# Banded attention in blocks of 32 queries by 64 keys instead of 64 by 96

## The chip, the cores and the metric

The kernel runs on one core of a Trainium2 chip. The metric is the time of one execution in microseconds on the device. A core has TensorE (PE in the profile; its weight loads are PEld), VectorE (DVE), ScalarE (ACT), GpSimd (POOL) and SyncE (SP), which issues the transfers here.

## What is computed

Attention with a band mask, then two mixing blocks on its output:

```python
scores = scale * np.matmul(q, k.transpose(0, 1, 3, 2))          # 4 batches, 8 heads, 576 positions, 64 dims
mask_plain = (rel >= 0) & (rel < window)                        # window 32, heads 0 to 3
mask_dil = (rel >= 0) & (rel < window * dilation) & (rel % dilation == 0)   # dilation 4, heads 4 to 7
...
attn = np.exp(scores - max); attn = attn / (sum + 1e-09); x = attn @ v
...
k = np.maximum(xk @ w_k, 0.0); v = k * k @ w_v; r = sigmoid(xr @ w_r); y = r * v    # xk, xr: x mixed with the row before
...
u = y + (y.T @ U @ V).T; out = u + np.maximum(u @ w_ch1, 0.0) @ w_ch2
```

A query sees at most 32 keys: itself and the 31 before it (in the dilated heads, every fourth position).

## The kernel before

The program records all its operations with a length in ns and what each reads and writes, and `plan` (lines 127 to 280) puts them in an order for each engine by simulating them as a list scheduler does. So a changed operation can move any other one.

The attention is cut into 32 units: a batch, a part of the sequence (320 or 256 positions) and a pair of heads. The first four units run alone (`attend`), the other 28 in 14 pairs (`attend2`): 6 pairs of the first part, with five windows a unit, and 8 of the second, with four. A window is 64 queries (QW) by 96 keys (KW). A pair goes through these steps:

- `qk` (line 654): scores, per unit x, window w and head e one fp32 matmul with 64 rows (the head's dims), 64 columns of weights (queries) and 96 moving columns (keys). Head e goes to PSUM bank `sc[e]`, a window to the upper or lower 64 partitions, so four 64x64 tiles of the array are in use. `attend` does the same with two tiles (line 545).
- `low` (665): VectorE adds the mask, scales and takes the row minimum, 96 columns an instruction; `exp` (673): ScalarE; `inv` (679, 680): VectorE; `norm` (684): GpSimd, one instruction a head.
- `tr` (699): each slot of 128 queries by 96 keys is transposed, five or four for each of the two heads. `copy` (351): ScalarE brings them from PSUM to SBUF, 512 columns and, with five windows, 128 more for each head.
- `pv` (716): per unit, window and head one matmul with 96 rows (keys), 64 columns of weights (V) and 64 moving columns (queries), in two tiles of 128x64. Then ScalarE copies the unit's output into x.

q and k come in one transfer a unit (line 522), V in another (525, 96 rows). A loop over the chunks of the first mixing block (`quanta`, three-pass matmuls at lines 816 to 818; the first chunk in fp32 at 813 and 829) calls `visit(2)` at two places a chunk, which starts the next pair's scores and ends the last pair's; so the attention's matmuls lie in groups among those of the mix. The fp32 matmuls of the first chunk need weights that VectorE and ScalarE convert from 64-bit words (lines 384 to 391). After some 300 us the attention is done, and the second mixing block (lines 1037 to 1116) follows.

Of the kernel before, what the change touches and what calls it, by code (L numbers as in the profile page):

```python
# [25 lines left out]
QW, KW = 64, 96  # L26
PARTS = ((0, 320), (320, 576))
WINDOWS = (5, 4)

NMASK = 6  # L30

TWO = ((0, 1), (0, 2), (3, 4))
NALL = NMASK + len(TWO)


def unit_kind(pair, part):

    if part == 0:
        return 5, 320, (0, 32, 96, 160, 224), (0, 1, 1, 1, 1) if pair < 2 else (0, 2, 3, 4, 5)
    if pair < 2:  # L40
        return 4, 288, (0, 64, 128, 192), (1, 1, 1, 1)
    return 4, 384, (0, 96, 192, 288), (1, 1, 1, 1)
# [34 lines left out]
def tile_attention_mix_channel(  # L77
    ctx: ExitStack, tc: tile.TileContext, qk0, qk1a, qk1b, v0, v1, cst, mu, w1raw, w2raw, upk, vpk, out
# [35 lines left out]
    def bank(tag):  # L114

        return Lazy([P, 512], F32, tag, f"ps{tag}", 4, ps)
# [394 lines left out]
    def a_load(u, which=("qk", "v")):  # L511
        b, part, pair = unit(u)
        nw, kc = unit_kind(pair, part)[:2]
        if part == 0:
            src, vsrc = qk0[b * NPAIR + pair], v0[b * NPAIR + pair]
        else:
            src, vsrc = (qk1a if pair < 2 else qk1b)[b * 2 + pair % 2], v1[b * NPAIR + pair]
        if u not in raws:
            raws[u] = Lazy([P, QKW + VW], F32, "raw", "raw", 4)
        raw = raws[u]  # L520
        if "qk" in which:
            load(P * 4 * (nw * QW + kc), lambda: nc.sync.dma_start(raw()[:, : nw * QW + kc], src),
                 (raw, "qk"), lambda: raw())
        if "v" in which:
            load(KW * 4 * 2 * nw * D, lambda: nc.sync.dma_start(raw()[:KW, QKW : QKW + 2 * nw * D], vsrc),
                 (raw, "v"), lambda: raw()[:, QKW:])

    def attend(u):
        b, part, pair = unit(u)
        nw, kc, starts, mk = unit_kind(pair, part)  # L530
        raw = raws.pop(u)
        sc, pr = bank("S"), Lazy([P, 512], F32, "pr", "pr", 4)
# [3 lines left out]
        t0, t1 = PARTS[part]  # L536
        fifth = slice(t1 - t0, t1 - t0 + P)
        pts = Lazy([P, 5 * P], F32, "pt", "pts", 2)

        def qk():  # L540
            for w in range(nw):
                for e in range(2):
                    r = slice(e * D, (e + 1) * D)
                    k0 = nw * QW + starts[w]
                    nc.tensor.matmul(
                        sc()[e * QW : (e + 1) * QW, w * KW : (w + 1) * KW],
# [3 lines left out]
        pe(nw * 168, qk, [(raw, "qk")], [(sc,)], "qk")  # L550
        yield

        def low():
            for w in range(nw):
                c = slice(w * KW, (w + 1) * KW)
                nc.vector.tensor_tensor_reduce(
                    out=pr()[:, c], in0=sc()[:, c], in1=masks[mk[w]], scale=-0.125, scalar=1.0e38,
                    op0=ALU.add, op1=ALU.min, accum_out=mn()[:, w : w + 1],
                )

        op("DVE", nw * 177, low, [(sc,), ("cst",)], [(pr,), (mn,)], 170)

        def exp():
            for w in range(nw):
                c = slice(w * KW, (w + 1) * KW)
                nc.scalar.activation(
                    pr()[:, c], pr()[:, c], AF.Exp, bias=mn()[:, w : w + 1], scale=-1.0, accum_out=sm()[:, w : w + 1]
                )

        op("ACT", nw * 360, exp, [(pr,), (mn,)], [(pr,), (sm,)], 190, mode="exp")  # L570

        def inv():
            nc.vector.tensor_scalar(sm()[:, :nw], sm()[:, :nw], 1e-9, None, op0=ALU.add)
            nc.vector.reciprocal(sm()[:, :nw], sm()[:, :nw])

        op("DVE", 260, inv, [(sm,)], [(sm,)], 80)

        def norm():
# [817 lines left out]
```

## Time and profile before

| | us |
|---|---|
| median of 3 runs | 775.47 (772.08 to 777.58) |
| the profiled execution | 775.23 |
| its span, first to last instruction | 773.3 |
| TensorE busy | 740.0 (96%) |
| VectorE busy | 580.5 (75%) |
| ScalarE busy | 404.8 (52%) |
| GpSimd busy | 396.1 (51%) |

The profile is of one execution. Busy time is the union of an engine's instructions; matmuls overlap in the pipeline, so what one costs is read from the start of one to the start of the next. The trace counts two records for an fp32 matmul and one for a transpose.

### The profile page before, as it was taken

The numbers are of one execution on the slowest core, as the hardware profiler recorded it, in microseconds if no ns is written. First come the engines' busy times: TensorE is split into PE (matmuls) and PEld (weight loads), VectorE is DVE, ScalarE is ACT, GpSimd is POOL, SyncE is SP. The second block draws the span as 40 slices with busy tenths as digits, with TensorE's granted clock in tenths as the row PEclk, the third lists the DMA queues.
The fourth block names the chain that finished last, engine by engine and source line by source line (L and its number), as shares of the span: only waits on it lengthen the run. The fifth ranks groups of instructions, "written<-read, shape, count | busy, mean of one in ns | idle before, by whom it ended". The sixth has DMA issues, their size and how long they took to land. (4 is left out here: it accounts for less than half of the span.)

```text
span 773.3 us, 16141 instructions
## 1 busy us (share of the span) xinstructions
PE 740.0 (96%) x5784; PEld 678.2 (88%) x5784; DVE 580.5 (75%) x1302; ACT 404.8 (52%) x1019; POOL 396.1 (51%) x404
## 2 busy tenths in 40 slices
PE   4798999999999999999999999999999999999998
PEld 3566899999999999999898899889988999898986
DVE  5889989999999963556467889876797974665632
ACT  4578778767767765454345444443544343333310
POOL 1333236455646564355367668544677754455600
PEclk9989999999999999999999999999999999999999
DMA  8677627759685720345652344123442312032001
GB/s 251 207 230 227 202 71 236 231 169 288 207 271 177 235 90 31 106 129 178 202 196 79 103 155 141 54 89 97 144 135 69 122 56 82 29 110 82 28 1 54
DMA packets 54255, 107.56 MB, mean 139 GB/s; under 512 B 5920, under 2 KB 16032, under 8 KB 54176
## 3 DMA queue, kind: packets, MB, share of 16 engines
q1 hardware_dynamic: 54176, 106.54, 42.8%
q8 instruction: 45, 0.74, 0.4%
q14 instruction: 34, 0.28, 0.1%
HBM read 83.97 MB, written 22.54 MB: 138 GB/s over the span
## 5 line engine op out<-in xcount | busy, mean ns | idle before, releaser
L346 POOL TENSOR_TENSOR cl<-sums,ch 128x512 fp32r<-128x512 f32 x72 | 99.6, 1383 | 82.5 <-ACT ch L351 57.2
L1116 PE MATMUL psS<-hl,rh 128*128 128x512 f32 (+1 forms) x320 | 119.5, 373 | 2.0 <-DVE hl L1052 2.0
L1114 PE MATMUL psS<-hh,rh 128*128 128x512 f32 (+1 forms) x320 | 119.5, 374 | 1.7 <-ACT hh L1051 0.9
L1115 PE MATMUL psS<-hh,rl 128*128 128x512 f32 (+1 forms) x320 | 119.0, 372 | 0.0
L351 ACT ACTIVATE ch<-sums 128x512 fp32r<-128x512 f32 (+1 forms) x104 | 57.1, 561 | 113.3 <-DVE sums L471 104.7
L816 PE MATMUL psM<-xk,wh 128*128 128x288 f32 x336 | 101.2, 301 | 0.4 <-DVE y L878 0.4
L817 PE MATMUL psM<-xk,wl 128*128 128x288 f32 x336 | 99.1, 295 | 0.0
L818 PE MATMUL psM<-xk,wh 128*128 128x288 f32 x336 | 98.8, 294 | 0.0
L471 DVE TENSOR_TENSOR sums<-st 128x256 f32<-128x256 f32 (+1 forms) x144 | 90.5, 675 | 8.7 <-POOL cl L346 5.9
L346 POOL TENSOR_TENSOR cl<-st,ch 128x256 fp32r<-128x256 f32 x80 | 68.8, 876 | 54.6 <-PE psM L1039 31.4
L346 POOL TENSOR_TENSOR xk<-m,xk 128x288 fp32r<-128x288 f32 x56 | 52.4, 949 | 50.6 <-ACT xk L351 39.9
L1116 PEld LDWEIGHTS psS<-hl,rh 128*128 128x128 f32 x320 | 60.3, 188 | 14.0 <-DVE hl L1052 2.4
L1114 PEld LDWEIGHTS psS<-hh,rh 128*128 128x128 f32 x320 | 60.3, 188 | 12.2 <-DVE us L950 1.1
L346 POOL TENSOR_TENSOR k2s<-k,k2s 128x288 fp32r<-128x288 f32 x49 | 44.0, 900 | 48.8 <-ACT k2s L351 47.5
L1115 PEld LDWEIGHTS psS<-hh,rl 128*128 128x128 f32 x320 | 60.3, 189 | 9.5
L816 PE MATMUL psM<-k2s,wh 128*128 128x288 f32 x224 | 67.5, 301 | 0.0
L817 PE MATMUL psM<-k2s,wl 128*128 128x288 f32 x224 | 66.0, 295 | 0.0
L818 PE MATMUL psM<-k2s,wh 128*128 128x288 f32 x224 | 65.9, 294 | 0.0
L816 PEld LDWEIGHTS psM<-xk,wh 128*128 128x128 f32 x336 | 63.0, 188 | 1.4 <-DVE y L878 0.9
L818 PEld LDWEIGHTS psM<-xk,wh 128*128 128x128 f32 x336 | 63.2, 188 | 0.0
L817 PEld LDWEIGHTS psM<-xk,wl 128*128 128x128 f32 x336 | 63.1, 188 | 0.1
L1074 DVE TENSOR_TENSOR ok<-ok,psM 128x256 f32<-128x256 f32 (+1 forms) x96 | 46.4, 503 | 20.3 <-PE psM L1039 18.5
(156 smaller groups left out, 2146.8 us busy)
## 6 DMA issues: line engine op xcount, KB each, us to landing
st<-w2f SPq DMA_DIRECT2D x96, 256.0 KB, 3.1
w<-w2raw SPq DMA_DIRECT2D x32, 512.0 KB, 5.2
w<-w1raw SPq DMA_DIRECT2D x20, 512.0 KB, 5.2
w2f<-w SPq DMA_DIRECT2D x32, 256.0 KB
raw<-qk SPq DMA_DIRECT2D x16, 320.0 KB, 4.5
ytmp<-y SPq DMA_DIRECT2D x32, 144.0 KB, 2.1
yb<-ytmp SPq DMA_DIRECT2D x4, 1152.0 KB, 6.4
uf<-us SPq DMA_DIRECT2D x32, 144.0 KB, 2.4
```

The costliest lines, as they stand in the source:

```text
L346: op("POOL", t, lambda: nc.gpsimd.tensor_tensor(out=out_(), in0=a(), in1=b(), op=ALU.subtract), r, w, 40, lock=True)
L351: act(n, lambda: nc.scalar.activation(out_(), in_(), AF.Copy), r, w, psum, strided)
L471: dve(k * Q, lambda: nc.vector.tensor_tensor(out=q(sm_, n, k)(), in0=a(), in1=b(), op=op_), [(s1,), (s2,)], [(sm_, key)], two=True)
L816: nc.tensor.matmul(a, lhsT=wh, rhs=xh, start=start, stop=False)
L817: nc.tensor.matmul(a, lhsT=wl, rhs=xh, start=False, stop=False)
L818: nc.tensor.matmul(a, lhsT=wh, rhs=xl, start=False, stop=stop)
L1074: dve(k * Q, lambda: nc.vector.tensor_tensor(out=out_(), in0=a(), in1=b(), op=op_), r, w, two=True, psum=True)
L1114: nc.tensor.matmul(a, lhsT=wh, rhs=xh, start=(j == 0 and e == 0), stop=False)
L1115: nc.tensor.matmul(a, lhsT=wl, rhs=xh, start=False, stop=False)
L1116: nc.tensor.matmul(a, lhsT=wh, rhs=xl, start=False, stop=(j == 7 and e == 1))
```

## The change

A window is 32 queries by 64 keys, so a unit has ten or eight. Scores go to 64x32 tiles (four windows of a head side by side on the 128 partitions), a slot of 128 queries holds four windows, and two slots of 64 keys make one 128x128 transpose that holds blocks of both units. The keys of unit 0 then stand on partitions 0 to 63 and those of unit 1 on 64 to 127, so PV runs in 64x64 tiles, and a pair's V comes in one transfer, unit 0's windows above unit 1's. The last two windows of a unit with ten share a slot between the heads; their masked minimum takes two instructions on 64 partitions each. Units that run alone transpose three blocks and copy them once, 384 columns wide. The masks are 5 x 64 columns in place of 9 x 96, so the constants' transfer is 448 columns instead of 992. The lengths that `plan` counts with are changed along with it.

```diff
-QW, KW = 64, 96
+QW, KW = 32, 64
...
-        return 5, 320, (0, 32, 96, 160, 224), (0, 1, 1, 1, 1) if pair < 2 else (0, 2, 3, 4, 5)
+            return 10, 320, (0,) + tuple(range(0, 288, 32)), (0, 1, 1)
...
 def attend(u):
-        copy(4 * P, lambda: pts()[:KW, : 4 * P], lambda: pt()[:KW], [(pt,)], [(pts, 0)], psum=True)
-        if nw == 5:
-            copy(P, lambda: pts()[:KW, 4 * P :], lambda: ov()[:KW, fifth], [(ov, "t")], [(pts, 1)], psum=True)
+        copy(3 * P, lambda: pts()[:, : 3 * P], lambda: pt()[:, : 3 * P], [(pt,)], [(pts, 0)], psum=True)
...
 def attend2(ua, ub):
-        raw = [raws.pop(ua), raws.pop(ub)]
+        rq, rv = raws.pop(("qk", ua // 2)), raws.pop(("v", ua // 2))
...
-                        sc[e]()[h * QW : (h + 1) * QW, slot * KW : (slot + 1) * KW],
-                        lhsT=raw[x]()[r, w * QW : (w + 1) * QW], rhs=raw[x]()[r, k0 : k0 + KW], start=True, stop=True,
-        pe(nw * 4 * 60, qk, [(x, "qk") for x in raw], [(x,) for x in sc], "qk")
+                        s_, h = (w // 4, w % 4) if w < 8 else (2, 2 * e + w - 8)
+                        c = (2 * s_ + x) * KW
+                            sc[e]()[h * QW : (h + 1) * QW, c : c + KW], lhsT=rq()[r, q0 : q0 + QW],
+                            rhs=rq()[r, k0 : k0 + KW], start=True, stop=True,
+        pe(nw * 4 * 28, qk, [(rq, x * QKW) for x in range(2)], [(x,) for x in sc], "qk")
...
+                for i in range(4):
+                    low(sc[e](), i * KW, pr(), base + (first_ + i) * KW, mk[i // 2], mn[e](), first_ + i)
+                if nw == 10:
+                    for f in range(2):
+                        low(sc[f](), (4 + e) * KW, pr(), base + own * KW, mk[2], mn[e](), own, head(f))
...
-                nc.tensor.transpose(dst, pr[e]()[:, w * KW : (w + 1) * KW], ident)
+                nc.tensor.transpose(to(i), pr()[:, i * P : (i + 1) * P], ident)
...
-            copy(4 * P, lambda e=e: pts[e]()[:KW, : 4 * P], lambda e=e: pt[e]()[:KW], [(pt[e],)], [(pts[e], 0)], psum=True)
+        copy(4 * P, lambda: pts()[:, : 4 * P], lambda: pt(), [(pt, 0), (pt, 1)], [(pts, 0)], psum=True)
...
-                        lhsT=raw[x]()[:KW, c : c + D], rhs=pts[e]()[:KW, slot * P + h * QW : slot * P + (h + 1) * QW],
+                        r = slice(x * D, (x + 1) * D)
+                            ov[x]()[e * D : (e + 1) * D, w * QW : (w + 1) * QW], lhsT=rv()[r, n : n + D],
+                            rhs=pts()[r, c : c + QW], start=True, stop=True,
```

The order of TensorE's instructions before, from the second pair of units on (psS is a PSUM bank of the attention, psM one of the mix, wx a converted weight, pr the exponentials, pts their transposes; an `x` counts matmuls):

```order
L813 MATMUL psM<-xk_248,wx 128x288 x16
L699 MATMUL psS<-cst_t,pr 96x128 x8
L716 MATMUL psS<-pts,raw 64x64 x16
L654 MATMUL psS<-raw 64x96 x20
...
L813 MATMUL psM<-k_615,wx 128x288 x16
L699 MATMUL psS<-cst_t,pr 96x128 x10
L716 MATMUL psS<-pts,raw 64x64 x20
```

And the same place now:

```order
L812 MATMUL psM<-xk_284,wx 128x288 x16
L714 MATMUL psS<-cst_t,pr 128x128 x4
L732 MATMUL psS<-pts,raw 64x32 x32
L676 MATMUL psS<-raw 32x64 x40
...
L714 MATMUL psS<-cst_t,pr 128x128 x5
L732 MATMUL psS<-pts,raw 64x32 x40
```

The groups keep their turn; a group has half the transposes and twice the score and PV matmuls, each with fewer columns.

ScalarE's first instructions before (x is the attention's output, w a raw weight):

```order
L566 ACTIVATE pr,sm<-pr,mn 128x96 x5
L384 ACTIVATE wx<-w_99 128x512
L351 ACTIVATE pts<-psS 96x512
L384 ACTIVATE wx<-w_132 128x512
L566 ACTIVATE pr,sm<-pr,mn 128x96 x5
L351 ACTIVATE pts<-psS 96x128
L351 ACTIVATE x_94<-psS 128x320
```

And now:

```order
L546 ACTIVATE pr,sm<-pr,mn 128x64 x5
L385 ACTIVATE wx<-w_99 128x512
L352 ACTIVATE pts<-psS 128x384
L385 ACTIVATE wx<-w_144 128x512
L546 ACTIVATE pr,sm<-pr,mn 128x64 x5
L352 ACTIVATE x_94<-psS 128x320
```

Unit 0's second copy of transposes, which stood behind the exponentials of unit 1, is gone.

## Rows read from the trace of the kernel before

**Rows 1.** The page's part 1: busy time, share of the span, instructions

```profile
PE 740.0 (96%) x5784; PEld 678.2 (88%) x5784; DVE 580.5 (75%) x1302; ACT 404.8 (52%) x1019; POOL 396.1 (51%) x404
```

**Rows 2.** Windows: length, busy time (instructions) of each engine, granted clock, DMA share, GB/s

```profile
0.00:20.00 20.00, 9.96 (x93) 7.96 (x94) 10.44 (x48) 10.21 (x39) 3.51 (x9) 0.89 0.81 251
...
60.00:270.00 210.00, 203.87 (x2010) 193.61 (x2009) 199.39 (x557) 156.12 (x454) 104.31 (x118) 1.00 0.67 210
270.00:360.00 90.00, 88.83 (x731) 86.20 (x729) 50.22 (x107) 49.87 (x115) 46.73 (x55) 1.00 0.30 98
```

**Rows 3.** Groups of TensorE by form: count, busy us, mean ns, idle before

```profile
L716 PE MATMUL psS<-pts,raw 96*64 96x64 f32 x496 | 19.3, 231 | 3.3 <-ACT pts L351 3.3
...
L699 PE MATMUL psS<-cst_t,pr 128*96 128x128 f32 x124 | 16.2, 273 | 2.9 <-POOL pr L684 2.9
...
L654 PE MATMUL psS<-raw 64*64 64x96 f32 x496 | 14.3, 258 | 0.0
```

**Rows 4.** Timeline of TensorE around three pairs: start, busy us, records

```profile
241.54 1.39 PE L716 MATMUL psS<-pts,raw 96*64 96x64 f32 x40
242.86 1.06 PE L654 MATMUL psS<-raw 64*64 64x96 f32 x40
243.84 0.40 PE L816 MATMUL psM<-k2s,wh 128*128 128x288 f32 x1
...
256.74 1.25 PE L699 MATMUL psS<-cst_t,pr 128*96 128x128 f32 x10
...
278.69 1.15 PE L716 MATMUL psS<-pts,raw 96*64 96x64 f32 x32
279.78 0.89 PE L654 MATMUL psS<-raw 64*64 64x96 f32 x32
280.60 0.40 PE L816 MATMUL psM<-k2s,wh 128*128 128x288 f32 x1
```

**Rows 5.** Timeline of TensorE, the second block's 128x128 transposes

```profile
510.89 0.60 PE L909 MATMUL psM<-cst_t,yb 128*128 128x128 f32 x4
```

**Rows 6.** Timeline of TensorE, units that run alone

```profile
22.51 1.04 PE L545 MATMUL psS<-raw 64*64 64x96 f32 x20
23.48 0.80 PE L603 MATMUL psS<-pts,raw 96*64 96x64 f32 x20
```

**Rows 7.** Timeline up to 221.71 us (PE) and 221.76 us (PEld), a score group's first records

```profile
221.68 0.31 PE L654 MATMUL psS<-raw 64*64 64x96 f32 x4
...
221.68 0.21 PEld L654 LDWEIGHTS psS<-raw 64*64 64x64 f32 x8
```

**Rows 8.** Timeline of VectorE, two masked minima in a row

```profile
60.63 0.25 DVE L665 CUSTOM_DVE_ANT_0 pr<-psS,cst_t 128x96 f32<-128x96 f32 x1
...
60.80 0.25 DVE L665 CUSTOM_DVE_ANT_0 pr<-psS,cst_t 128x96 f32<-128x96 f32 x1
```

**Rows 9.** Groups of ScalarE by form

```profile
L351 ACT ACTIVATE pts<-psS 96x512 f32<-96x512 f32 x32 | 17.4, 585 | 8.0 <-PE psS L590 4.4 <-PE psS L699 3.5
```

**Rows 10.** Timeline of the start, ScalarE and TensorE

```profile
12.09 0.59 ACT L351 ACTIVATE pts<-psS 96x512 f32<-96x512 f32 x1 [3.72 <-PE psS L590]
...
14.92 0.26 ACT L351 ACTIVATE pts<-psS 96x128 f32<-96x128 f32 x1
...
16.66 0.44 ACT L351 ACTIVATE x<-psS 128x320 f32<-128x320 f32 x1 [1.48 <-PE psS L603]
...
18.50 4.08 PE L829 MATMUL psM<-xk,wx 128*128 128x288 f32 x8
...
72.00 6.57 PE L813 MATMUL psM<-k,wx 128*128 128x288 f32 x26 [2.92 <-DVE wx L391]
```

More of the change, by code (lines that the diff above doesn't have):

```diff
@@ L524, in a_load, with tile_of @@
-        if "v" in which:
-            load(KW * 4 * 2 * nw * D, lambda: nc.sync.dma_start(raw()[:KW, QKW : QKW + 2 * nw * D], vsrc),
-                 (raw, "v"), lambda: raw()[:, QKW:])
+        src = qk0[b * NPAIR + pair] if part == 0 else (qk1a if pair < 2 else qk1b)[b * 2 + pair % 2]
+        alone = u < NPAIR
+        at_ = 0 if alone else pair % 2 * QKW
+        def tile_of(key):
+            if key not in raws:
+                raws[key] = Lazy([P, 2 * QKW], F32, "raw", "raw", 4)
+            return raws[key]
@@ new lines, in a_load @@
+        if "qk" in which:
+            raw = tile_of(u if alone else ("qk", u // 2))
+            load(P * 4 * (nw * QW + kc), lambda: nc.sync.dma_start(raw()[:, at_ : at_ + nw * QW + kc], src),
+                 (raw, at_), lambda: raw()[:, at_:])
+        if "v" in which and alone:
+            rv = tile_of(u)
+            load(P * 4 * nw * D, lambda: nc.sync.dma_start(rv()[:, QKW : QKW + nw * D], v0[u]), (rv, "v"), lambda: rv()[:, QKW:])
+        elif "v" in which and pair % 2:
+            vt = tile_of(("v", u // 2))
+            vsrc = v0p[(b - 1) * 2 + pair // 2] if part == 0 else v1p[b * 2 + pair // 2]
+            load(P * 8 * nw * D, lambda: nc.sync.dma_start(vt()[:, : 2 * nw * D], vsrc), (vt, "v"), lambda: vt())
@@ L548, in qk @@
                     )
-        pe(nw * 168, qk, [(raw, "qk")], [(sc,)], "qk")
+        pe(nw * 2 * 40, qk, [(raw, 0)], [(x,) for x in sc], "qk")
         yield
[L553 to L574, printed above, removed]
@@ L630, in attend2 @@
         b, part, pair = unit(ua)
-        nw, kc, starts, _ = unit_kind(pair, part)
-        mk = ((6, 1, 6, 1, 1) if pair < 2 else (7, 8, 7, 8, 5)) if part == 0 else (1, 1, 1, 1)
-        raw = [raws.pop(ua), raws.pop(ub)]
+        nw, kc, starts, mk = unit_kind(pair, part)
+        rq, rv = raws.pop(("qk", ua // 2)), raws.pop(("v", ua // 2))
         sc = [bank("S") for _ in range(2)]
-        pr = [Lazy([P, 512], F32, "pr", "pr", 4) for _ in range(2)]
+        pr = Lazy([P, 10 * KW], F32, "pr", "pr", 4)
@@ new lines, in attend2, with to, tr @@
+        yield
+        def to(i):
+            if nw == 8:
+                return pt()[:, i * P : (i + 1) * P]
+            return ov[0]()[:, fifth] if i == 2 else pt()[:, (i - i // 3) * P : (i - i // 3 + 1) * P]
+        def tr(some):
+            for i in some:
+                nc.tensor.transpose(to(i), pr()[:, i * P : (i + 1) * P], ident)
+        pe(2 * 108, lambda: tr((0, 1)), [(pr, 0), ("cst",)], [(pt, 0)], "tr")
+        rest = range(2, ns)
+        pe(len(rest) * 108, lambda: tr(rest), [(pr, 0), (pr, 1), ("cst",)], [(pt, 1)] + ([(ov[0], "t")] if nw == 10 else []), "tr")
@@ L742, in attend2 @@
+        pe(nw * 4 * 30, pv, [(pts, k) for k in range(nw // 2 - 3)] + [(rv, "v")], [(x,) for x in ov], "pv")
+        yield
+        for x in range(2):
+            x_out(ov[x], pair + x, part, b)
         yield
```

280 lines of the change are left out of this document (129 added, 151 removed).

## The prediction

> **What bounds the kernel now.** I read the page's first two parts first. TensorE is busy 740.0 of 773.3 us, no other compute engine above 75% [rows 1], and the granted clock is 1.00, its upper level of 2.4 GHz, from 60 us on [rows 2]. So the end is set by how much TensorE has to do and by its few idle stretches, not by a chain through the other engines. The windows then say where the slack is: from 60 to 270 us, where nearly all of the attention is done between the matmuls of the channel mix, TensorE is busy 203.9 of 210 us, and VectorE with 199.4 stands right behind it; from 270 to 360 us VectorE drops to 50.2 of 90 [rows 2]. In the first 20 us TensorE is busy half the time. A nanosecond of TensorE work saved after 60 us is therefore worth nearly a nanosecond, as long as VectorE can follow; in the start it is worth nothing by itself.
>
> What the attention costs TensorE I take from starts, not from busy times, which overlap. An fp32 matmul leaves two records, a transpose one: 124 transposes, and 496 records each for scores and PV [rows 3], which is 14 pairs of units, 6 with five windows (10 transposes, 40 records of each kind) and 8 with four (8, 32 and 32).
>
> **The change part by part.** *Transposes.* Ten in a row are busy 1.25 us [rows 4] with 0.27 us for the last one [rows 3]: (1.25 - 0.27)/9 = 0.109 us each. They are now 128x128 instead of 128x96. The kernel has transposes of that size already: four take 0.60 us [rows 5], (0.60 - 0.27)/3 = 0.110, the same. A pair needs half as many, 62 go: 62 x 0.109 = **-6.8 us**. Nothing covers this work; TensorE runs it between full matmuls.
>
> *Scores.* From the first score matmul of a five-window pair to the next matmul of another kind are 0.98 us for 40 records, for a four-window pair 0.82 us for 32 [rows 4]: 0.16/8 = 20 ns a record and 0.18 us of entry and exit. A lone unit, whose blocks use only two tiles of the array, needs 0.97 us for 20 records, some 49 ns [rows 6]. Twice the tiles halve the time of a record, so tiles run beside each other, and a record holds its own 64x64 tile for 4 x 20 = 80 ns at 96 columns. A transpose holds the array 109 ns for 128 columns, so 32 columns are worth about 29 ns; 64 columns come to 51 ns by that, and a PV record of 64 columns takes 58 (below). I take 55. There are now twice as many records (80 and 64), but the tiles are 64x32, eight of them. The fullest tile gets 6 matmuls in a five-window pair (the last two windows of both units fall on the same four tiles) and 4 in the other: 12 x 55 ns + 0.18 = 0.84 us (-0.14) and 8 x 55 ns + 0.18 = 0.62 us (-0.20). Sum 6 x 0.14 + 8 x 0.20 = **-2.4 us**. This needs a record started every 7 ns. That the engine can start them so is in the trace: four score matmuls begin within 0.03 us and eight weight loads within 0.08 us [rows 7]. That it keeps this up over 80 records no row shows; the upper bound is the 20 ns of today (rival 3).
>
> *PV.* 1.32 us for 40 records, 1.09 for 32 [rows 4]: 29 ns a record, 0.16 us aside, so 58 ns in each of two 128x64 tiles. Now there are 80 (64) records with half the moving columns in four 64x64 tiles: again 20 (16) records on each tile. If a record is paced by its weight load (still 64 columns), it stays at 58 ns and PV costs 1.32 and 1.09 us as before, **0**; if by its columns, it falls to 58 - 29 = 29 ns, and 6 x 0.58 + 8 x 0.47 = 7.2 us more go. I take 0, since the 58 lie above what the columns explain (51), and keep the other end for the range.
>
> At this place the Trainium skill, "TensorEngine Tiling (Array Packing)", Performance Considerations, speaks against the change: it gives each matmul about 60 cycles of overhead, so that one with few moving columns lasts as long as one with 60, and warns against tiling away a dimension that is already small. 60 cycles at 2.4 GHz are an estimate of 25 ns; if they followed one another, 80 + 80 records would cost 4.0 us a pair instead of 2.3. The score records of today, at 20 ns apart over four tiles, already run below that, so the overhead cannot be a serial one.
>
> *VectorE, ScalarE, GpSimd, DMA.* The masked minimum starts every 0.18 us for 96 columns [rows 8]. For 64 it lies between 0.12 (all in proportion) and 0.18; I take 0.15. A five-window pair has 12 now for 10 (0 us), a four-window pair 8 for 8: 8 x 8 x 0.03 = 1.9 us less. ScalarE's exponentials keep their number and get shorter, and one 512-wide copy of 0.585 us [rows 9] goes in each pair; GpSimd normalises 640 columns a pair instead of 960 (512 for 768). All three leave the bound alone and only widen slack. V grows from 96 to 128 rows, 0.1 to 0.2 MB a pair; the DMA engines are busy 67% between 60 and 270 us [rows 2], so I cost it at nothing; without that cover it would be about 2 MB at the 210 GB/s of that row, 10 us of transfer spread over 14 pairs, none of it waited for.
>
> *The start.* Unit 0's copies to SBUF run at 12.09 and, behind five exponentials, at 14.92; then PV, the copy of x at 16.66 and the first matmul of the mix at 18.50 [rows 10]. Now it is one copy, so PV need not wait for a second one. But the stretch ends on the weights' conversion: TensorE waits 2.92 us for it as late as 72.00 [rows 10], and the conversions are as many as before. So of the 2 to 3 us I count 1; bounds are 3 less and, since the plan puts all rows of the start in a new order, 3 more.
>
> **Sum.** 6.8 + 2.4 + 0 = 9.2 us less for TensorE, about 8 of it between 60 and 300 us. VectorE, minus its 1.9, then stands at 197.5 of some 202 us there: closer than before, so I give back 2 us to waits of TensorE for it. With 1 us from the start: 775.2 (profiled execution: span 773.3 and 1.9 around it) - 9.2 + 2 - 1 = **767.0 us**. The median of the runs, 775.5, is 0.3 us away and moves nothing.
>
> **The rivals.**
> 1. *VectorE becomes the bound.* For it: 95% busy from 60 to 270 us. Against: TensorE's 6 idle us there show no large waits for it, and after 270 us it has 40 us to spare for work that can slip. Then only VectorE's 1.9 us and the start's 1 us arrive: 772.3.
> 2. *Only four score tiles run at once.* No row shows more than four. A record then costs 55/4 = 14 ns: 80 x 14 + 0.18 = 1.30 and 64 x 14 + 0.18 = 1.08 us, +0.32 and +0.26 a pair, 4.0 us in all. TensorE saves 6.8 - 4.0 = 2.8, with the start 771.4.
> 3. *The records set the time (slower).* If a record takes its 20 ns however many tiles there are, scores cost 80 x 0.020 + 0.18 = 1.78 and 1.46 us, PV 1.76 and 1.44: +1.24 a pair with five windows, +0.99 with four. Less the transposes (0.55 and 0.44) that is 6 x 0.69 + 8 x 0.55 = 8.5 us: 783.7. It decides from 15.7 ns a record: 160 records and 0.34 us against 0.98 + 1.32 + 0.55. For it: 20 ns is the shortest sustained pace in the trace. Against: the starts 7 ns apart.
> 4. *PV is paced by its columns.* 767.0 - 7.2 = 759.8. Against: the 58 ns.
>
> **How the numbers follow.** My forecast 0.50, rival 1 0.15, rival 2 0.17, rival 3 0.12, rival 4 0.06. A measurement of this kernel tells 1% (7.8 us) from no change; the lines are 767.7 and 783.2. The forecast lies just beyond the first one, spread 4 us to each side by the start and by the giving back: 0.30 of its 0.50 is faster, the rest within 1%. With rival 4 and what strays from 1 and 2 (0.08), faster is 0.44. Rival 3 and what the new order could lose give slower 0.13, and 0.43 stays within. The range goes from rival 4, 759, past rivals 1 and 2, to 780, short of the worst of rival 3.
>
> **What would show it.** In the profile after: 62 pair transposes about 0.11 us apart; a five-window pair's scores 0.84 us from start to the next kind, PV 1.32. Scores of 1.30 mean rival 2, of 1.78 rival 3; PV of 0.74 means rival 4. TensorE's idle time from 60 to 270 us above 8 us, released by VectorE, means rival 1. The forecast is wrong if these blocks shrink as said and the end doesn't move, or if the first stretch (to the first three-pass matmul of the mix) grows by over 3 us.

## The result: slower by 1.25%, with blocks that got cheaper

The changed kernel takes 785.7 us (median of 4 runs, 780.7 to 786.9) against 775.1 us, a ratio of 1.0125 (95% interval 1.0093 to 1.0158). 767.0 was forecast, with 759 to 780 as the range. Part 1 of the page after:

```profile
PE 740.2 (95%) x6866; PEld 677.0 (86%) x6866; DVE 563.9 (72%) x1334; ACT 394.8 (50%) x995; POOL 386.1 (49%) x408
```

The span is 782.9 us (773.3). TensorE is busy as long as in [rows 1], 740.2 against 740.0, and stands idle 42.7 us instead of 33.3 (span less busy): nearly all of the 9.6 us of difference between the spans is idle time. That the busy time did not fall needs explaining too, since the blocks did shrink. First the blocks, in the timeline of TensorE, to set beside [rows 4]:

```profile
217.53 1.14 PE L732 MATMUL psS<-pts,raw 64*64 64x32 f32 x64
218.59 0.86 PE L676 MATMUL psS<-raw 64*32 64x64 f32 x64
219.38 0.40 PE L815 MATMUL psM<-xk,wh 128*128 128x288 f32 x1
...
249.38 0.71 PE L714 MATMUL psS<-cst_t,pr 128*128 128x128 f32 x5
249.84 0.38 PE L815 MATMUL psM<-k2s,wh 128*128 128x288 f32 x1
...
251.73 1.37 PE L732 MATMUL psS<-pts,raw 64*64 64x32 f32 x80
253.03 1.08 PE L676 MATMUL psS<-raw 64*32 64x64 f32 x80
254.04 0.40 PE L815 MATMUL psM<-k2s,wh 128*128 128x288 f32 x1
```

Read from start to start. Five transposes take 0.46 us where ten took about twice that; PV takes 1.30 and 1.06 us (1.32 and 1.09 before); scores 1.01 and 0.79 us (0.98 and 0.82). A pair is cheaper by 5 x 0.109 + 0.02 - 0.03 = 0.53 us with five windows and 4 x 0.109 + 0.03 + 0.03 = 0.50 us with four: 6 x 0.53 + 8 x 0.50 = 7.2 us in all. What ate them are the windows (columns as in [rows 2]):

```profile
0.00:20.00 20.00, 9.68 (x173) 7.58 (x174) 9.96 (x53) 9.75 (x37) 3.98 (x12) 1.00 0.75 246
60.00:270.00 210.00, 196.23 (x2565) 185.32 (x2552) 197.31 (x564) 141.93 (x415) 100.66 (x114) 0.98 0.67 218
270.00:360.00 90.00, 89.05 (x960) 86.70 (x959) 44.91 (x122) 51.76 (x129) 42.90 (x55) 1.00 0.27 88
...
40.00:100.00 60.00, 46.88 (x583) 36.10 (x582) 50.32 (x152) 39.46 (x118) 17.99 (x21) 0.89 0.62 203
46.40:53.20 6.80, 5.25 (x11) 3.83 (x12) 6.70 (x12) 4.65 (x9) 3.40 (x4) 0.50 0.51 178
```

and the same stretch of the kernel before:

```profile
40.00:100.00 60.00, 54.21 (x435) 43.53 (x434) 58.19 (x159) 49.33 (x135) 20.31 (x21) 0.95 0.68 216
```

In the timeline of TensorE before, the first three-pass matmul and the first one of the channel block (L1037) are

```profile
90.36 0.51 PE L816 MATMUL psM<-xk,wh 128*128 128x288 f32 x1
...
366.19 0.28 PE L1037 MATMUL psM<-tr,ch 128*128 128x256 f32 x1
```

From 40 to 100 us TensorE is busy 7.3 us less and VectorE 7.9, and the granted clock is 0.89 instead of 0.95. The timeline of TensorE after shows where:

```profile
47.95 9.16 PE L812 MATMUL psM<-xk,wx 128*128 128x288 f32 x26 [4.17 <-DVE wx L392]
...
67.06 8.15 PE L812 MATMUL psM<-xk,wx 128*128 128x288 f32 x26 [4.45 <-DVE wx L392]
...
79.23 1.37 PE L732 MATMUL psS<-pts,raw 64*64 64x32 f32 x80 [3.47 <-ACT pts L352]
...
99.04 0.38 PE L815 MATMUL psM<-xk,wh 128*128 128x288 f32 x1
...
373.43 0.28 PE L1036 MATMUL psM<-tr,ch 128*128 128x256 f32 x1
```

Three waits of 3.5 to 4.5 us from 40 to 100 us, where before had one of 2.92 [rows 10]. In the first of them the clock falls to 0.50 (1.2 GHz, 46.4 to 53.2 us, last row of the windows), and the same 26 matmuls that take 6.57 us in [rows 10] take 9.16. So the wait costs twice, and the longer busy time hides what the blocks save: over the whole trace TensorE is at 1.2 GHz for 23.9 us, before for 13.7. The first three-pass matmul comes 8.7 us late, the channel block 7.2 us late; the end of the run adds 2.4, with no more idle time than before (8.3 and 8.4 us) but 3.4 us at 1.2 GHz from 421.9 us on. Why VectorE was late itself is in the rows of ScalarE:

```profile
49.41 0.67 ACT L385 ACTIVATE wx<-w 128x512 f32<-128x512 f32 x1
...
53.15 0.41 ACT L857 ACTIVATE rt<-psM 128x288 f32<-128x288 f32 x1 [2.12 <-PE psM L812]
...
55.21 0.41 ACT L857 ACTIVATE rt<-psM 128x288 f32<-128x288 f32 x1 [1.17 <-PE psM L812]
...
57.15 0.41 ACT L857 ACTIVATE rt<-psM 128x288 f32<-128x288 f32 x1 [1.06 <-PE psM L812]
...
57.94 0.58 ACT L352 ACTIVATE pts<-psS 128x512 f32<-128x512 f32 x1
58.41 1.24 ACT L385 ACTIVATE wx<-w 128x512 f32<-128x512 f32 x2
```

and of VectorE:

```profile
59.11 0.43 DVE L386 TENSOR_SCALAR wx<-wx 128x512 f32<-128x512 f32 x1 [5.17 <-ACT wx L385]
```

The eleventh weight conversion (L385 at 58.41; 49.0 us before) stands in ScalarE's row behind copies that wait for TensorE, which runs at the low clock after its wait for the conversion before. The transfer of that raw weight was issued as early as before (43.77 us, before 43.42), so it is the place in the row that is late. Each engine works in its fixed order, so the three wait for each other in a ring.

### The profile page after: what moved, and what is told of

It reads as the page before. It is cut to its first block, busy times and chain, and to the rows that moved or that the text cites. A ratio compares the mean times of both kernels' runs of the same rounds, so it can differ in the third digit from the quotient of the medians.

```text
span 782.9 us, 18285 instructions
## 1 busy us (share of the span) xinstructions
PE 740.2 (95%) x6866; PEld 677.0 (86%) x6866; DVE 563.9 (72%) x1334; ACT 394.8 (50%) x995; POOL 386.1 (49%) x408
## 4 chain that ended last, share of the span: by engine, by line
PE 73%; DVE 13%; DMA 4%; issue 3%; ACT 3%; POOL 2%; SPq 0%; DVEq 0%; POOLq 0%; ACTq 0%
PE psS L1115 8%; PE psS L1113 8%; PE psS L1114 8%; PE psM L1036 7%; PE psM L1038 7%; PE psM L1037 7%; PE psM L815 7%; PE psM L816 6%; PE psM L817 6%; PE psS L732 2%; PE psS L676 1%; PE psM L812 1%; DVE pr L537 1%; DVE sums L472 1%; PE psM L828 1%
## 5 line engine op out<-in xcount | busy, mean ns | idle before, releaser
L347 POOL TENSOR_TENSOR cl<-st,ch 128x256 fp32r<-128x256 f32 x80 | 65.5, 836 | 56.0 <-PE psM L1038 32.3
L472 DVE TENSOR_TENSOR sums<-st 128x256 f32<-128x256 f32 (+1 forms) x144 | 86.5, 651 | 5.0 <-POOL cl L347 3.8
L347 POOL TENSOR_TENSOR k2s<-k,k2s 128x288 fp32r<-128x288 f32 x49 | 46.5, 948 | 58.1 <-ACT k2s L352 56.3
L1114 PEld LDWEIGHTS psS<-hh,rl 128*128 128x128 f32 x320 | 60.5, 189 | 10.6 <-DVE rl L349 1.1
L1093 DVE SCALAR_TENSOR_TENSOR hl<-ort,hh 128x512 fp32r<-128x512 f32 x32 | 26.8, 836 | 50.1 <-ACT hh L1092 49.1
```

Of the source, the lines that this page charges most:

```text
L347: op("POOL", t, lambda: nc.gpsimd.tensor_tensor(out=out_(), in0=a(), in1=b(), op=ALU.subtract), r, w, 40, lock=True)
L472: dve(k * Q, lambda: nc.vector.tensor_tensor(out=q(sm_, n, k)(), in0=a(), in1=b(), op=op_), [(s1,), (s2,)], [(sm_, key)], two=True)
L1114: nc.tensor.matmul(a, lhsT=wl, rhs=xh, start=False, stop=False)
```

## Experiments

Two hypotheses lead: **A**, the loss is in the order that the planner made anew; **B**, it is in the blocks themselves. A third, **C**, lays it to the single V transfer of a pair. Each ratio below is against the kernel before on the same chip, and the places of single matmuls are from each run's profile.

**Exchange of orders.** The planner's passes are replaced by a table with a place for every operation, taken from the other kernel's order:

```diff
-        rank, order, end = None, None, None
-        for _ in range(PASSES):
...
+        left, order = sorted(ops, key=lambda o: PLACE_AT[o.i]), []
+        while left:
+            o = next(o for o in left if ready(o) is not None)
+            left.remove(o)
+            order.append(o)
```

> The changed blocks (32 by 64, their transposes and PV), issued in the order that the planner made for the kernel before: every operation outside attention, and each attention step, stands on each engine where it stood before; the pair's single V transfer stands where the second unit's V transfer stood. Theory A (the loss comes from the order that the planner made anew, whose weight conversions come late on ScalarE in the start): the first three-pass matmul of the mix starts near 90 us, as before, not near 99, and with about 0.5 us saved in each of 12 pairs the time is 768 us, between 764 and 772. Theory B (the new blocks themselves cost, in their records, their VectorE pieces or the shorter chain of one pair): the time stays near 785 us, whatever the order. Theory C (the one V transfer of a pair, which waits for a buffer, holds up the queue of the weight loads): the weight loads are late here too, the first three-pass matmul near 96 us or later, and the time 778 us or more.

Measured: 772.4 us, ratio 0.9949 (0.9932 to 0.9967), at the upper end of what A expected. The timeline of TensorE:

```profile
57.47 0.54 PE L676 MATMUL psS<-raw 64*32 64x64 f32 x15 [3.14 <-issue]
...
89.10 0.51 PE L815 MATMUL psM<-xk,wh 128*128 128x288 f32 x1
...
360.82 0.28 PE L1036 MATMUL psM<-tr,ch 128*128 128x256 f32 x1
```

> The reverse: the blocks of before (64 by 96, two V transfers a pair), issued in the order that the planner made for the changed kernel. Theory A (the order): the start is late as in the changed kernel, first three-pass matmul near 99 us, and with the dearer blocks the time is 785 to 793 us. Theory B (the new blocks): 775 us, as before, within 3. Theory C (the one V transfer): the start is as before, near 91 us, and the time 775 to 780 us, since the V transfers are two again.

Measured: 798.3 us, ratio 1.0263 (1.0222 to 1.0304), worse than expected. Its timeline:

```profile
51.81 9.54 PE L813 MATMUL psM<-xk,wx 128*128 128x288 f32 x26 [5.29 <-DVE wx L391]
...
71.37 8.26 PE L813 MATMUL psM<-xk,wx 128*128 128x288 f32 x26 [4.04 <-DVE wx L391]
...
84.71 2.07 PE L716 MATMUL psS<-pts,raw 96*64 96x64 f32 x40 [3.99 <-ACT pts L351]
...
388.01 0.28 PE L1037 MATMUL psM<-tr,ch 128*128 128x256 f32 x1
```

The three waits belong to the order: old blocks have them in it, new blocks don't have them in the old one. What the order costs the new blocks up to the first three-pass matmul is in two windows, of the changed kernel and of the new blocks in the old order (columns as in [rows 2]):

```profile
0.00:99.04 99.04, 72.12 (x1007) 54.84 (x1007) 75.92 (x261) 59.26 (x190) 26.94 (x40) 0.91 0.69 227
```

```profile
0.00:89.10 89.10, 65.74 (x1002) 49.82 (x1002) 73.54 (x253) 56.43 (x173) 25.13 (x38) 0.98 0.73 242
```

With nearly the same matmuls in both, TensorE is idle 26.9 us against 23.4 and busy 72.1 against 65.7, at 1.2 GHz for 17.1 us against 3.4. So of the 9.9 us that the start loses, 3.5 are idle time and 6.4 are busy time, which the lower clock lengthens. B falls. So does C (the single V transfer): the start in the old order is 1.3 us sooner than before with that transfer in place. In an equal order the new blocks begin the channel block sooner by 5.4 us (old order: 360.82 against 366.19) and 14.6 us (new: 373.43 against 388.01), so in a poor order what the blocks bring is not only their own 7.2 us.

A second exchange: four planner numbers changed in both kernels,

```diff
-CONV0 = [min(20, 7 + n) for n in range(20)]
-WINDOW = 160
-SLACK = 100.0
-SLACK_PE = 100.0
-PASSES = 10
+CONV0 = [min(20, 6 + n) for n in range(20)]
+WINDOW = 180
+SLACK = 130.0
+SLACK_PE = 150.0
+PASSES = 20
```

and the new blocks then put in the order which that gives the old ones.

> The changed kernel with four numbers of its planner changed (it looks 180 operations ahead, its slack is 130 ns and 150 ns on TensorE, the conversions of the mix begin one sooner in the program, 20 passes), which gives another order of the same instructions: a second draw beside the one with 200 operations. If the order that the planner happened to make is what costs (theory A), this one too is well below 785.7 us: 767 to 775 us. If the new blocks cost whatever the order, except in that of before and one other, 780 us or more.

> The kernel before with the same four numbers of its planner changed as in the run of the changed kernel that came to 771.0 us: a control for whether these numbers or the new blocks gave that time. If the new blocks save some 4 us in equal orders, as the exchange of orders has it, this one takes 774 to 782 us; if the numbers did it and the blocks are worth nothing, 769 to 773 us.

> The new blocks in the order that the planner with the four changed numbers made for the kernel before, which took 772.6 us with the old blocks and 771.2 us in its profile. A second exchange of orders. If the new blocks save in an equal order what they did in the first exchange, 0.5% or 4 us against the old blocks, this is 766 to 770 us and the best of all runs; if that saving was luck of the first exchange, 771 to 776 us.

Measured: new blocks in their own order 771.0 us (0.9945, 0.9923 to 0.9966); old blocks 772.6 us (0.9945, 0.9919 to 0.9970), which by what was expected meant that the numbers did it and the blocks are worth nothing; new blocks in the old blocks' order 765.6 us (0.9870, 0.9840 to 0.9900), the best of all runs and faster than both kernels. There the channel block begins at 360.71 us against 366.28 with the old blocks: 5.6 us, as in the first exchange. So the blocks are worth something in this order too; in their own order with these numbers they showed none of it.

**Other orders of the same instructions.** One number or a set of lengths in the planner changed at a time:

```diff
-WINDOW = 160
+WINDOW = 200
...
-SLACK = 100.0
+SLACK = 80.0
...
-GATED = 28
+GATED = 26
...
-        pe(nw * 4 * 28, qk, [(rq, x * QKW) for x in range(2)], [(x,) for x in sc], "qk")
+        pe(nw * 120, qk, [(rq, x * QKW) for x in range(2)], [(x,) for x in sc], "qk")
```

> The changed kernel with one number of its planner changed: it looks 200 operations ahead, not 160, so that it makes another order for the same instructions. Theory A, in the form that the order of the changed kernel is a poor one among many: the time moves by several us, most likely down, to 770 to 782 us, with fewer microseconds in which TensorE waits before its first three-pass matmul than the 27 of the changed kernel. Theory B and theory C (the blocks, or the V transfer): another order does not help, 783 to 788 us.

> The kernel before with one number of its planner changed (the slack within which an urgent operation may be put first, 80 ns in place of 100), so that it makes another order for the same instructions: a control for what any new order does. If orders differ by several us among themselves, this one is 3 us or more from 775 us on either side (776 to 785 us is the likelier side, since 775 us is the better of the two orders seen so far); if an order made by this planner is as good as another, it stays within 3 us of 775 us, and theory A needs a reason that lies in the new blocks.

> The changed kernel in an order of its own, planned with the lengths that the kernel before gave to the attention steps (a pair's scores, transposes, PV, masked minima, exponentials and normalising as long as with 64 by 96 blocks); the instructions are the same. Theory P (the planner made a poor order because the attention is now cheaper in its model): this order is like the two borrowed from the old blocks, the channel block begins at 359 to 363 us and the time is 764 to 773 us. Theory L (any new order is a draw; the one of the changed kernel was a bad draw): somewhere between 766 and 790 us, and the channel block 363 us or later as in the three own orders so far (365.8, 366.4, 373.4).

> The changed kernel in an order of its own with one number changed: the rule that a transfer waits for the fourth one before it holds for the first 26 transfers, not 28. With one V transfer a pair in place of two, that rule had come to reach two more weight transfers than before. Theory G (that rule made the weights late): the eleventh conversion on ScalarE begins near 50 us, not 58, the waits of over 4 us for VectorE's wx go, the first three-pass matmul comes before 93 us and the time is 768 to 774 us. Theory L (a bad draw): the eleventh conversion is earlier as planned, but the time is like that of any other draw, 766 to 790 us, with other waits of 2 us and more in the start.

> The changed kernel in an order of its own with one number of its planner changed, the same one as in the control on the kernel before (slack 80 in place of 100), which there moved nothing (775.7 against 775.6 us). Theory L: another draw between 766 and 790 us; with the four own orders beside it, it shows how far draws lie apart. If the new blocks bring a poor order as a rule, 780 us or more.

| order | us | ratio (95%) | first three-pass matmul at, us | channel block at, us | TensorE idle up to there, us |
|---|---|---|---|---|---|
| old blocks, own (the kernel before) | 775.1 | 1 | 90.4 | 366.2 | 24.9 |
| old blocks, slack 80 | 775.7 | 0.9990 (0.9967 to 1.0012) | 96.6 | 367.9 | 26.2 |
| new blocks, own (the changed kernel) | 785.7 | 1.0125 (1.0093 to 1.0158) | 99.0 | 373.4 | 34.4 |
| new blocks, window 200 | 772.6 | 0.9958 (0.9933 to 0.9983) | 102.4 | 366.4 | 28.8 |
| new blocks, slack 80 | 778.7 | 1.0034 (1.0013 to 1.0055) | 92.3 | 369.1 | 33.9 |
| new blocks, gate 26 | 780.8 | 1.0064 (1.0037 to 1.0092) | 95.7 | 368.6 | 34.3 |
| new blocks, old lengths | 776.0 | 0.9993 (0.9963 to 1.0023) | 91.3 | 366.7 | 32.6 |

With the two exchanges' rows, six own orders of the new blocks run from 0.9945 to 1.0125, around no change; three of the old blocks from 0.9945 to 1. Theory L (a draw) fits all of them, within the wide range that it gave. But the control on the old blocks stayed within 3 us, which by its expectation sends theory A to look for a reason in the new blocks, so the width of the draws is shown for the new blocks alone.

The first three-pass matmul does not tell the time of an order. With window 200 it came at 102.4 us, later than in the changed kernel, after 27.2 us of idle time where fewer than 27 were expected, and the time was 772.6 us all the same:

```profile
102.41 0.51 PE L815 MATMUL psM<-xk,wh 128*128 128x288 f32 x1
```

With the four other numbers it came at 98.0 us, for 771.0 us. In both, TensorE is idle only 1.6 and 2.2 us from there to the channel block, in the changed kernel 7.5. What goes with the time is TensorE's idle time up to the channel block: the six own orders of the new blocks have 26.7 (the four other numbers), 28.8, 32.6, 33.9, 34.3 and 34.4 us, in the order of their times.

Theory P falls, since the old lengths brought 366.7, not 359 to 363. Theory G falls in its price: the eleventh conversion does begin sooner (50.8 us), but a wait of 4.82 us for wx comes all the same, and 780.8 us is a poor draw.

**Only the weight conversions moved.** The table of places holds the kernel's own order, but for the last 13 conversions, which take the other kernel's planned times; that table, in place of the planner's passes, is the whole edit. The transfers of the raw weights move with their conversions.

> The changed kernel in its own order but for one thing: the last 13 of the 20 weight conversions of the start (each a transfer, a ScalarE step and three VectorE steps) stand where the planner had them by its own clock in the kernel before, up to 8 us sooner (the eleventh by the most). On TensorE hardly a row moves. Theory A1 (the new order is poor because its weight conversions stand late in ScalarE's and VectorE's rows, TensorE then waits for weights and its clock falls): the two waits of over 4 us for VectorE's wx shrink under 2 us each, the first three-pass matmul of the mix comes at 92 to 96 us, not 99, and the time falls from 785.7 to 775 to 781 us. Theory A2 (the place of the conversions is only a sign of a poor order; what TensorE waits for is the attention steps that stand around them): VectorE and ScalarE have their waits elsewhere, TensorE waits as long for others, and the time stays at 783 to 788 us.

Measured: 789.4 us, 1.0202 (1.0143 to 1.0261), no faster than the changed kernel (1.0093 to 1.0158), and outside what either theory expected. TensorE in the profiled execution, the longest of four (796.5 us):

```profile
48.61 8.26 PE L812 MATMUL psM<-xk,wx 128*128 128x288 f32 x26 [3.69 <-DVE wx L392]
...
67.57 9.19 PE L812 MATMUL psM<-xk,wx 128*128 128x288 f32 x26 [5.44 <-DVE wx L392]
...
83.79 2.36 PE L732 MATMUL psS<-pts,raw 64*64 64x32 f32 x80 [6.49 <-ACT pts L352]
```

ScalarE there, the fifteenth conversion of the start:

```profile
65.80 0.66 ACT L385 ACTIVATE wx<-w 128x512 f32<-128x512 f32 x1 [3.77 <-DMA w<-w1raw]
```

> The reverse, in the kernel before (its own blocks and order): the last 13 of the 20 weight conversions of the start stand where the planner had them by its own clock in the changed kernel, up to 8 us later. Theory A1 (late conversions are what the new order costs): TensorE waits for VectorE's wx 6 to 10 us more in the start, its clock falls there, the first three-pass matmul comes at 95 to 100 us (before 90.4), and the time is 779 to 786 us. Theory A2 (a sign only): 773 to 778 us, as before.

Measured: 794.7 us, 1.0253 (1.0214 to 1.0293), far more than either theory gave; TensorE:

```profile
64.75 9.56 PE L813 MATMUL psM<-xk,wx 128*128 128x288 f32 x26 [3.77 <-DVE wx L391]
...
80.61 1.33 PE L813 MATMUL psM<-k,wx 128*128 128x288 f32 x2 [5.33 <-DVE wx L391]
```

A1 holds in one direction alone. Late conversions do cost. Set early, they did not mend the order: the two waits for wx stayed (3.69 and 5.44 us) and the one for pts grew from 3.47 to 6.49. The trace has a reason, the raw weights: ScalarE waits for their transfers for 16.7 us in all, in the changed kernel for 2.6, and the exponentials that stand behind in its row wait with it. So in this run the conversions stood ahead of their transfers, and what early conversions are worth whose weights have landed it does not show.

**What sets the start.** VectorE's work is cut (m is 64 columns of 512 in the clamp and the shift), nothing is moved:

```diff
-        dve(n, lambda: nc.vector.tensor_scalar(x(), x(), HI_MIN, HI_MAX, op0=ALU.max, op1=ALU.min), kx, kx)
+        dve(n, lambda: nc.vector.tensor_scalar(x()[:, :m], x()[:, :m], HI_MIN, HI_MAX, op0=ALU.max, op1=ALU.min), kx, kx)
...
-        cv_bits(raw, CW, whole_w[at])
+        cv_bits(raw, CW, whole_w[at], 64 if len(whole_w) > 7 else None)
```

> The kernel before, its own order, where the last 13 weight conversions of the start do the first two of their four VectorE steps (the clamp and the shift) on 64 columns in place of 512; so these weights are not the reference's. That takes some 0.65 us a piece, 8 us in all, from VectorE before the first three-pass matmul, and nothing from another engine. Theory V (VectorE, busy 58.2 of the 60 us from 40 to 100, sets the pace of the start, and an order is as good as it keeps VectorE fed): the first three-pass matmul comes 5 to 9 us sooner, at 81 to 86 us, and the time is 766 to 771 us. Theory S (ScalarE's row and TensorE's waits set it, and VectorE only follows): 88 to 91 us, and 773 to 777 us.

Measured: 771.6 us, 0.9933 (0.9905 to 0.9961). Its window and, in the timeline, its first three-pass matmul:

```profile
40.00:100.00 60.00, 57.45 (x464) 47.23 (x463) 53.74 (x165) 50.70 (x141) 20.18 (x23) 0.95 0.67 216
```

```profile
86.14 0.51 PE L816 MATMUL psM<-xk,wh 128*128 128x288 f32 x1
```

Between the theories, nearer to V: the first three-pass matmul comes 4.2 us sooner, about half of what was taken from VectorE. So VectorE's work sets part of the pace of the start, not all of it.

**Records and instructions.** In the first exchange TensorE stood still for 3.14 us in the middle of a score group, with "issue" as the cause: nothing that the profile shows. More records should show whether they set the time:

```diff
-                        nc.tensor.matmul(
-                            sc[e]()[h * QW : (h + 1) * QW, c : c + KW], lhsT=rq()[r, q0 : q0 + QW],
-                            rhs=rq()[r, k0 : k0 + KW], start=True, stop=True,
-                        )
+                        for s in (0, 32):
+                            nc.tensor.matmul(
+                                sc[e]()[h * QW : (h + 1) * QW, c + s : c + s + 32], lhsT=rq()[r, q0 : q0 + QW],
+                                rhs=rq()[r, k0 + s : k0 + s + 32], start=True, stop=True,
+                            )
```

> The new blocks in the order of before (772.4 us), with each 32 by 64 score matmul of the pairs issued as two of 32 columns: the same columns in all, twice the records (160 in a pair of ten windows, 128 in one of eight). The 80 records of such a pair took 1.01 us in the changed kernel. If the number of records sets the time of the scores (about 10 ns each when eight tiles work at once), they take 1.9 to 2.1 us in a pair of ten windows, and the time rises by 6 to 11 us to 778 to 783 us, since the pairs lie on TensorE's path. If the columns set it, as the prediction had it, they take 1.0 to 1.2 us and the time is 772 to 774 us.

Measured: 803.3 us, 1.0389 (1.0327 to 1.0452), 31 us above the exchange where 6 to 11 were expected. The group of the scores (busy, mean ns, idle before and its cause):

```profile
L677 PE MATMUL psS<-raw 64*32 64x32 f32 x1984 | 25.3, 201 | 21.1 <-issue 21.1
```

Two pairs in the timeline of TensorE:

```profile
152.93 1.71 PE L677 MATMUL psS<-raw 64*32 64x32 f32 x152
159.38 0.43 PE L677 MATMUL psS<-raw 64*32 64x32 f32 x8 [4.74 <-issue]
...
180.25 1.77 PE L677 MATMUL psS<-raw 64*32 64x32 f32 x160
181.95 0.40 PE L816 MATMUL psM<-k2s,wh 128*128 128x288 f32 x1
```

The DMA queues from 157.0 to 158.2 us (packets, MB, share of 16 engines):

```profile
q1 hardware_dynamic: 186, 0.43, 94.1%
q8 instruction: 1, 0.02, 5.0%
```

160 records take 1.70 us where 80 of twice the columns took 1.01: a record costs 10.6 ns against 12.6, so the number of records, not of columns, sets nearly all of it (1.9 to 2.1 us was expected for that, 1.0 to 1.2 if the columns did). The Trainium skill, "TensorEngine Tiling (Array Packing)", Performance Considerations, puts an overhead of about 60 cycles on each matmul, an estimate of 25 ns at 2.4 GHz, and warns against tiling away a dimension that is already small. As a distance from one matmul to the next the trace does not show that overhead over eight tiles; the warning it bears out. The stops are new: 21.1 us of them at the scores. In the one shown, the group breaks off 8 records before its end while the queues are 94% busy with data, one transfer of instructions lands at 158.05 us, and TensorE goes on 1.3 us later. In the traces of all runs with the new blocks there are 22 such stops of over 0.25 us, and each ends 1.2 to 1.6 us after an instruction transfer of this queue landed; with the old blocks there is none. The page counts the transfers: 45 before, 54 after, 62 here. After most of the stops the clock is low for some us too: up to the channel block TensorE is at 1.2 GHz for 37.6 us here, in the exchange for 3.4. So a stop costs more than its length; how the 31 us divide among stops, clock and records is not shown.

> The kernel before, its own order, with each 64 by 96 score matmul of the pairs issued as two of 48 columns: the same arithmetic and tiles, but as many score records in a pair as the changed kernel has (80 and 64). In all the kernels with the old blocks TensorE never stood still at the scores for a cause that the trace does not show (issue); with the new blocks it did for 0.4 to 6.4 us in all, and with the new scores halved for 43 us counted on both of its rows. Theory I (TensorE's instructions come to the chip in pieces, and a pair with over 150 score instructions empties what is there): such waits appear here too, 2 to 8 us in all, the instruction transfers of the page go from 45 to 54, and the time rises by 3 to 9 us, to 778 to 784 us. Theory J (it is the small tiles, 32 by 64, that stall): no such wait, 45 to 54 transfers, and 774 to 777 us.

The same edit in the kernel before, with 48 columns. Measured: 777.4 us, 1.0013 (0.9989 to 1.0037); no stop, 49 transfers. A pair's scores took 1.42 us (58.11 to 59.53) for 0.98, some 0.4 us more in each of 14 pairs, and still the time did not move: time added to TensorE there was not paid in full either. By its wording theory J is nearer, but the dose was smaller than meant (49 transfers, and over four tiles 80 records take longer). The four transfers more came with 993 more instructions in the trace, the eight more of the halved scores with 1984, so it is TensorE's instructions that this queue brings. The next run tells them apart: the scores of a pair no longer stand right behind the PV of the last,

```diff
-        join(old + new)
+        join(old or new)
+        join(new if old else [])
```

> The run with the halved scores (803.3 us) with one difference: the scores of a new pair, which stood directly behind the PV of the pair before (64 or 80 PV records and 128 or 160 score records in one piece), stand two TensorE operations of the mix later, 8 matmuls of the first stage or 6 to 12 three-pass matmuls each. Nothing is removed. Theory I (TensorE uses up instructions faster there than they come, and stops until the next transfer of them has landed): the stops for no cause the trace shows fall from 21.7 us to under 6 us, and the time from 803 us to 780 to 790 us. Theory J (the small score tiles themselves stall): the stops stay within a few us of 21 us, and so does the time, 798 us or more.

Measured: 799.1 us, 1.0312 (1.0277 to 1.0348). The same group, with the same instructions and the same 62 transfers:

```profile
L677 PE MATMUL psS<-raw 64*32 64x32 f32 x1984 | 23.4, 200 | 0.8 <-issue 0.8
```

The stops are gone but for one, 21.1 to 0.8 us: theory I, supply of instructions, and J falls. But the time hardly follows, which theory I did not expect. From the first three-pass matmul to the channel block TensorE now waits 11.7 us for other engines (y, k and pts above all), where beside the stops it had waited 1.4; the stops had covered these waits or the later scores made them, the runs do not tell which.

> The new blocks in the order of before (772.4 us), with the scores of a pair set two TensorE operations of the mix behind the PV of the pair before, as in the run with halved scores. Theory I: the 3.6 us that TensorE stopped for instructions there go, and the time falls by 2 to 4 us to 768 to 771 us, unless the later scores make the pair's VectorE and ScalarE steps late in the start, which could give back as much (772 to 775 us). Theory J: the stops stay, 772 us or more.

Measured: 790.9 us, 1.0198 (1.0165 to 1.0231), 18 us worse than with the scores in place; no stop at the scores. The first three-pass matmul moves from 89.1 to 99.9 us, again in an order that was only touched. The window up to it:

```profile
0.00:99.94 99.94, 77.96 (x1001) 57.74 (x1002) 72.85 (x250) 57.79 (x175) 26.64 (x38) 0.85 0.65 217
```

It has no more idle time than the exchange, 22.0 us against 23.4, but TensorE is busy 78.0 us against 65.7 with the same matmuls, and at 1.2 GHz for 30.7 us against 3.4. So in the start the loss is the clock. It is not chance of one execution: the mean granted clock of the six executions is 0.979 to 0.985, of the exchange's ten 0.985 to 0.997. Why it falls, with waits no longer than there, no run shows. From this run to the halved scores in the same places it is 8 us, near the price of 80 (64) more records a pair.

## Why the prediction was wrong

**Transposes: right.** 62 of them 0.11 us apart; -6.8 us.

**PV: right in size.** "I take 0": 1.30 and 1.06 us, against rival 4's 0.74, so the columns do not pace it. That the weight load does, as the prediction had it, is not shown: no run changes the weights alone.

**Scores: mis-sized.** "I take 55" ns for a record in its tile. (Its 29 ns for 32 columns is 27 by the 109 ns it comes from, and 64 columns are 53, not 51; neither moves the 55.) The 7 ns between starts is there within a burst, in the timeline of the changed kernel's TensorE up to 253.10 us:

```profile
253.03 0.29 PE L676 MATMUL psS<-raw 64*32 64x64 f32 x8
```

Eight records start within 0.07 us, and the group takes 1.01 us, not rival 2's 1.30, which falls. But the pace does not last: the ninth starts 80 ns after the first, and 80 records take 1.01 us, not 0.84. The term is 0 in place of -2.4 us. Rival 3's 20 ns a record did not come true, yet its mechanism is there at 10.6 to 12.6 ns, below its 15.7 ns.

**"A nanosecond of TensorE work saved after 60 us is therefore worth nearly a nanosecond": too much.** Of 7.2 us saved in the pairs, the two exchanges into an order made for the old blocks show 5.4 and 5.6 at the channel block, and over the whole run 0.5% and 0.75%, 4 to 6 us. (In the order of the changed kernel it is 1.3%; there TensorE's idle time up to the channel block fell too, from 39.2 to 34.4 us.) Part of the rest are stops for instructions, 3.14 us in one group of the first exchange and 2.64 in a wait of the other; no term of the sum had them.

**The new order: the step that failed.** "Of the 2 to 3 us I count 1; bounds are 3 less and, since the plan puts all rows of the start in a new order, 3 more." The same blocks take 785.7 us in the new order and 772.4 in the old one, so the order cost 13.3 us, over four times that bound. The start came 8.7 us later, by more than the 3 us that the prediction had named as a sign of being wrong, and up to the channel block TensorE was idle 34.4 us in place of 24.9 and ran at 1.2 GHz for 20.5 in place of 13.7. I had priced unit 0's copies and left the order of all other rows to a bound, and to the start alone; the sum has no term for the clock. The sign itself was not a good one, since orders with an equally late start took 771.0 and 772.6 us.

How poor the order came out was bad luck in part: it is the slowest of six own orders, which lie 14 us apart with equal instructions (0.9945 to 1.0125). Two of the six lie above the range's 780 us. One is slower by over 1%, five are within 1% and none is faster by 1%, so the chance of 0.13 for slower was about right, and the 0.44 for faster too high. In the order of before the new blocks came to 772.4 us, in that of the second exchange to 765.6, on the two sides of the forecast.

**Rival 1** (VectorE the bound) is half right, in another place. From 60 to 270 us TensorE was idle 13.8 us, above the 8 us of its sign, but VectorE released 4.7 of them, ScalarE 4.3 and GpSimd 3.9. In the start VectorE and ScalarE's row feed TensorE, and work taken from VectorE there came back in part (771.6 us).

**Open.** Borrowed orders began the channel block at 360.7 and 360.8 us, six own orders at 365.8 to 373.4. Neither the lengths nor the gate explains why the planner does worse for the new blocks by itself; that may be chance in so few draws. What decides when the clock falls is open too: a wait of 2.1 us at 25 to 26 us ended at 1.2 GHz in the run with the scores moved and at 2.4 GHz in the exchange.

## What to carry to other kernels

When a change passes through a scheduler, it changes two things, the instructions and the order. Run the new instructions in the old order, and the old in the new, before judging either: here the instructions were worth -0.5 to -1.3%, and the order +1.8% with the new blocks and +2.6% with the old. Where engines work through fixed rows and wait for each other in a ring, draw several orders and keep the best; setting one late step sooner did not help here, since ScalarE then waited for its transfer. Compare orders at one place late in the run, here the channel block, and not by when one early step begins. And count records: halving a matmul past the point where the records set the time saves nothing and uses up instructions twice as fast.

## What the runs showed of the hardware

TensorE can run out of instructions: in or up to 3.3 us behind groups of 128 to 240 PV and score records in a row, most of them at 12 to 14 ns each, it stopped for 0.3 to 4.7 us, 22 times, and each time went on 1.2 to 1.6 us after an instruction transfer had landed; in the stop shown, data transfers filled the queues to 94%. With long matmuls between PV and scores the same records stopped once, for 0.8 us.

Over eight 64x32 tiles a score record costs 12.3 to 12.6 ns with 64 columns and 10.6 to 10.9 with 32 (the groups of 64 and 80 records take 0.79 and 1.01 us, of 128 and 160 records 1.40 and 1.70), so columns hardly count there.

A wait of 4.17 us came with 6.8 us at 1.2 GHz, and the 26 matmuls behind it took 9.16 us instead of 6.57. And an order can lose by the clock alone: with 30.7 us at 1.2 GHz in place of 3.4, the same matmuls kept TensorE busy 78.0 us in place of 65.7, and the start was 10.8 us longer with 1.4 us less idle time.
